# A second feed-forward stage whose token loads, weight loads and one subtraction are issued elsewhere

## The chip, the cores and the metric

The kernel runs on one core of one Trainium2 chip. The metric is the device time of one execution in microseconds (us). Three executions of the kernel before took 1824.18, 1825.57 and 1827.65 us; the median is 1825.57 us.

## The reference

Three stages follow each other. Attention over 8 x 8 heads with keys and values averaged in groups of 8 gives 4608 token vectors of 512 numbers. A first feed-forward network (512 to 2048 to 512) follows. The second one, around which the change lies, is:

```python
rms = np.sqrt(np.mean(x * x, axis=-1, keepdims=True) + 1e-06)
xn = x / rms * rms_g
g = xn @ w_gate
silu = g * (1.0 / (1.0 + np.exp(-g)))
val = xn @ w_val
return (silu * val @ w_out).astype(np.float32)
```

Here x is 4608 x 512, w_gate and w_val are 512 x 1536 and w_out is 1536 x 512, all in float32.

## The kernel before

Every float32 operand of a matmul is split into a high and a low part (helper `split`, L88 to L95: the high part is a copy on ScalarE, the low part a subtraction on an engine that the caller names), and a product is three matmuls.

The second network starts some 980 us into the span and treats the tokens in five pairs of two token blocks: pairs 0, 2 and 4 with 512 tokens in a block, pairs 1 and 3 with 384. For a pair, the products with w_gate ("g") and w_val ("v") are done by twelve **quads** (class `Quad`): six pairs of column blocks p, each first for g and then for v. A quad multiplies 2 x 2 blocks with seven block products (Strassen's scheme) in the steps p1, p6, p5, p2, p7, p4, p3; each step is six matmuls. p1 of the next quad is put ahead of p4 and p3. A quad uses three banks of PSUM: x (p1, p2), y (p6, p7, p4) and w (p5, p3). Results leave the banks through VectorE and ScalarE; in a g quad ScalarE applies Silu, in a v quad VectorE and GpSimd multiply and split.

The product with w_out (`out_part`, L1089) is cut in **pieces**, two for each of its twelve row blocks f and each token block z. Those of z = 0 are put between the quads' steps by `piece()`, one behind p7 and one behind p3; those of z = 1 follow the last quad, and the last four of them go into the first two quads of the next pair. Four banks take the sums; the copies out (`oe`) must leave a bank before z = 1 writes it.

Weights come from device memory, all issued by the SyncE queue (SP), in order: an instruction whose buffer is not yet left holds up all that is behind it. A quad needs four tiles `a` (`load_a`, L956) out of ten slots: tile 0 is read by p1 and p2, tile 1 by p6 and p5, tile 2 by p7 and p3, tile 3 by p4. So in quad i the load of a tile ten further on takes the slot of a tile of quad i. w_out comes as tiles `wo` (`load_o`, L966) in four slots, issued by a piece three blocks ahead of its use.

While a pair is being multiplied, the next pair's tokens are loaded and normalised in small steps (`norm_steps`), one behind each of p6, p5, p2 and p7 (`between`). For each of its two blocks z: `load` (tile `xst`, L832), four `square` (ScalarE, sums on GpSimd into `acc`, L844 to L848), `mean` (`acc` split into the tile `ahl`), empty steps, `root` (two matmuls `ms` with a matrix of ones, L857, then Sqrt on ScalarE, L860, which changes ScalarE's function table and back), `inverse` (VectorE, L864) and `scaled` (VectorE, L868). For the first pair the same steps run in the last tile of the first network, four at a time.

Within the second network every engine executes in the order in which the code issues (a chain of dependencies, L1220 on, sees to it); in the first network a scheduler may reorder.

Of the kernel before, what the change touches and what calls it, by code (L numbers as in the profile page):

```python
# [16 lines left out]
HI, LO = 0, 1  # L17
# [5 lines left out]
def pooled_attention_then_two_ffns(  # L23
# [13 lines left out]
    nc = tc.nc  # L37
# [6 lines left out]
    KC = DM // P  # L44
# [24 lines left out]
    def bank(tag, bufs, name):  # L69
        return ps.tile([P, 512], F32, tag=tag, bufs=bufs, name=name)  # L70
# [18 lines left out]
    def split(hi_eng, hi, lo_eng, lo, src):  # L89

        if hi_eng is nc.scalar:
            nc.scalar.activation(out=hi, in_=src, func=AF.Copy)  # L92
        else:
            hi_eng.tensor_copy(out=hi, in_=src)
        lo_eng.tensor_tensor(out=lo, in0=src, in1=hi.bitcast(F32), op=ALU.subtract)  # L95
# [11 lines left out]
    class Weights:  # L107
# [51 lines left out]
        def step(self):  # L159
            if self.begun:  # L160
                self.end()
            while self.todo and len(self.loaded) < self.ahead(self.todo[0]):
                self.load()
            if self.loaded:
                self.begin()
# [640 lines left out]
    def slot(kind, i, name):  # L806

        base, n = {
            "t": (0, T_SLOTS), "a": (T_SLOTS, A_SLOTS), "o": (T_SLOTS + A_SLOTS, O_SLOTS),
            "u": (T_SLOTS + A_SLOTS + O_SLOTS, F2),  # L810
        }[kind]
        return weight_slot(free2[base + i % n], name)

    def norm_steps(q):

        t0, n = pairs[q]
        xs = []
        steps = []

        def wait():  # L820
            pass

        for z in range(2):
            ta = t0 + z * n

            def load(z=z, ta=ta):
                x = p2.tile([P, KC, N], F32, tag="xst", bufs=2, name=f"xst{q}_{z}")[:, :, :n]
                xs.append(x)
                at_ = ta
                while at_ < ta + n:  # L830
                    end = min(ta + n, (at_ // N + 1) * N)
                    nc.sync.dma_start(  # L832
                        out=x[:, :, at_ - ta:end - ta],
                        in_=y_dram[at_ // N][:, :, at_ % N:at_ % N + end - at_],
                    )
                    at_ = end

            held = {}

            def square(c, z=z, held=held):  # L840
                x = xs[z]
                if c == 0:
                    held["acc"] = p2.tile([P, N], F32, tag="acc", bufs=1, name=f"acc{q}_{z}")[:, :n]
                    nc.scalar.activation(out=held["acc"], in_=x[:, c, :], func=AF.Square)  # L844
                else:
                    s = per.tile([P, N], F32, tag="tg", bufs=3, name=f"sq{q}_{z}_{c}")[:, :n]
                    nc.scalar.activation(out=s, in_=x[:, c, :], func=AF.Square)
                    nc.gpsimd.tensor_tensor(out=held["acc"], in0=held["acc"], in1=s, op=ALU.add)  # L848

            def mean(z=z, held=held):  # L850
                held["a"] = p2.tile([P, 2, N], F32R, tag="ahl", bufs=1, name=f"ahl{q}_{z}")[:, :, :n]
                split(nc.scalar, held["a"][:, HI, :], nc.gpsimd, held["a"][:, LO, :], held["acc"])

            def root(z=z, held=held):
                pt = bank("h", 2, f"ms{q}_{z}")[:, :n]
                for i in range(2):
                    nc.tensor.matmul(pt, ones, held["a"][:, i, :], start=i == 0, stop=i == 1)  # L857
                r = p2.tile([P, N], F32, tag="rms", bufs=1, name=f"rms{q}_{z}")[:, :n]
                held["r"] = r
                nc.scalar.activation(out=r, in_=pt, func=AF.Sqrt, bias=eps)  # L860

            def inverse(c, held=held):
                r = held["r"]
                nc.vector.reciprocal(out=r[:, c:c + P], in_=r[:, c:c + P])  # L864

            def scaled(c, z=z, held=held):
                x = xs[z]
                nc.vector.scalar_tensor_tensor(  # L868
                    out=x[:, c, :], in0=x[:, c, :], scalar=gain[:, c:c + 1], in1=held["r"],
                    op0=ALU.mult, op1=ALU.mult,  # L870
                )

            steps.insert(z, load)

            steps += [wait] + [lambda c=c, f=square: f(c) for c in range(KC)] + [mean, wait, wait, root, wait]
            steps += [lambda c=c, f=inverse: f(c) for c in range(0, n, P)]
            steps += [lambda c=c, f=scaled: f(c) for c in range(KC)]
        return xs, steps
# [67 lines left out]
    def load_a():  # L946
        if a_count[0] < len(a_todo):
            i = a_count[0]
            a_count[0] += 1
            if len(a_todo[i]) == 3:  # L950
                load_o_into(a_todo[i], "a", i)
                return
            q, p, m, s = a_todo[i]
            t = slot("a", i, f"a{m}{q}_{p}_{s}")
            k = 2 if s < 3 else 1
            nc.sync.dma_start(  # L956
                out=t.rearrange("p h n -> p (h n)")[:, :k * 512].bitcast(F32),
                in_=op_dram[m, p][:, s, 0:k].rearrange("p a c n -> p (a c n)"),
            )
            a_tiles[q, p, m, s] = t.rearrange("p h n -> p (h n)").rearrange(  # L960
                "p (a c h n) -> p a c h n", a=2, c=2, h=2
            )

    def load_o_into(key, kind, i):
        t = slot(kind, i, f"wo{key[0]}_{key[1]}_{key[2]}")
        nc.sync.dma_start(out=t.bitcast(F32), in_=wo_dram[key[2]])  # L966
        o_tiles[key] = t
# [6 lines left out]
    def first_pair():  # L974

        xs, norm = norm_steps(0)
        early, late = token_steps(0, xs)
        when = {}
        for i, x in enumerate(norm):
            when.setdefault(i // 4, []).append(x)  # L980
        first = (len(norm) - 1) // 4 + 1
        for i, x in enumerate(early):
            when.setdefault(first + i, []).append(x)
        for i in range(A_SLOTS):
            when.setdefault(10 + i // 2, []).append(load_a)
        for i in range(3):
            when.setdefault(13 + i // 2, []).append(load_o)
        return when, late
# [173 lines left out]
    def piece():  # L1162
        if pieces:
            pieces.pop(0)()

    def queue_out(q, z, f):
        for ms in ((0, 1), tuple(range(2, pairs[q][1] // P))):
            def one(ms=ms):
                if ms[0] == 0:
                    load_o()  # L1170
                    if (q, z) == (last_q, 1):
                        load_a()
                out_part(q, z, f, ms)
            pieces.append(one)

    begun = len(nc.cur_bb.bb.instructions)
    for q, (_, n) in enumerate(pairs):
        quads = [Quad(q, p, m) for p in range(NPAIR) for m in "gv"]
        more = q + 1 < len(pairs)
        xs, norm = norm_steps(q + 1) if more else (None, [])  # L1180

        def between():
            load_a()
            if norm and i >= 2:
                norm.pop(0)()

        for i, a in enumerate(quads):
            if i == 0:
                a.p1()
            for step in (a.p6, a.p5, a.p2, a.p7):  # L1190
                step()
                between()
            piece()
            if i + 1 < len(quads):
                quads[i + 1].p1()
            a.p4()
            a.p3()

            if i + 1 < (len(quads) if more else len(quads) - 2):
                piece()  # L1200
            if a.m == "v":
                for f in (2 * a.p, 2 * a.p + 1):
                    queue_out(q, 0, f)
        assert not norm
        while pieces:
            piece()
        for f in range(F2):
            queue_out(q, 1, f)
        early, late = token_steps(q + 1, xs) if more else ([], [])

        for i in range(len(pieces) - (4 if more else 0)):
            if i % 3 == 0 and early + late:
                (early or late).pop(0)()
            piece()
        assert not early + late
# [40 lines left out]
```

## Time and profile before

| | |
|---|---|
| median of three runs | 1825.57 us |
| the profiled execution | 1826.16 us |
| its span, first to last instruction | 1824.4 us |
| TensorE matmul busy (PE) | 1764.8 us, 97% |
| VectorE (DVE) / ScalarE (ACT) / GpSimd (POOL) busy | 881.1 / 669.4 / 557.0 us |
| DMA moved | 330.81 MB, mean 181 GB/s |
| mean granted TensorE clock | 0.992 |

The first three rows say that a term read in the trace can be taken off the profiled execution's own time, 1.8 us above its span and 0.6 us above the median. PE is busy nearly always; the busy time of a matmul runs into that of the next, so a wait shows best in the distance between the starts of two steps. The second network takes the last 843 us of the span.

### The profile page before, as it was taken

How to read it: one execution, taken by the hardware profiler on the slowest of the kernel's cores; microseconds unless marked ns; L12 is line 12 of the kernel's file. 1: busy time of each engine (PE TensorE's matmuls, PEld its weight loads, DVE VectorE, ACT ScalarE, POOL GpSimd, SP SyncE). 2: the span in 40 equal slices, each digit the busy share in tenths (PEclk: the TensorE clock that was granted, in tenths of full speed). 3: DMA queues.
4: the chain of work that ended last, by engine and by line, in shares of the span. 5: the costliest groups of instructions: out<-in, count | busy, mean ns of one | idle time of the engine just before them, and what ended most of it. 6: DMA issues, size and time to landing. Idle time of an engine off the chain costs nothing.

```text
span 1824.4 us, 23632 instructions
## 1 busy us (share of the span) xinstructions
PE 1764.8 (97%) x8596; PEld 1504.5 (82%) x8596; DVE 881.1 (48%) x1593; ACT 669.4 (37%) x1424; POOL 557.0 (31%) x691
## 2 busy tenths in 40 slices
PE   4899999999999999999999999999999999999999
PEld 3789887888888887888888878989787888988887
DVE  8974445463356555554244336344534533463331
ACT  5754334343343444343433332233232223322220
POOL 2653204243124252111211442244144114513330
PEclk9999999999999999999999999999999999999999
DMA  8832105446365445445442657687676567776562
GB/s 266 292 118 85 47 21 159 151 150 222 104 192 161 157 147 161 144 143 165 159 150 82 230 175 247 188 294 245 237 248 207 187 221 281 247 264 201 197 208 104
DMA packets 175556, 330.81 MB, mean 181 GB/s; under 512 B 54352, under 2 KB 90192, under 8 KB 174928
## 3 DMA queue, kind: packets, MB, share of 16 engines
q1 hardware_dynamic: 175440, 329.31, 54.9%
q8 instruction: 68, 1.11, 0.3%
q14 instruction: 48, 0.39, 0.1%
HBM read 277.87 MB, written 51.38 MB: 180 GB/s over the span
## 4 chain that ended last, share of the span: by engine, by line
PE 87%; DVE 4%; DMA 4%; POOL 2%; issue 1%; ACT 1%; SPq 1%; ACTq 0%; DVEq 0%; POOLq 0%
PE h L592 20%; PE y L628 20%; PE o L1089 14%; PE yv L1014 6%; PE yg L1014 6%; PE xv L1014 4%; PE wv L1014 4%; PE wg L1014 4%; PE xg L1014 4%; PE sc L325 2%; DMA wo<-wo 1%; PE av L395 1%; DMA xst<-y 1%; PE xt L369 1%; PE qt L303 1%
## 5 line engine op out<-in xcount | busy, mean ns | idle before, releaser
L592 PE MATMUL h<-xhl,w_i 128*128 128x512 f32 (+1 forms) x1824 | 438.6, 386 | 3.0 <-ACT xhl L92 1.5
L592 PEld LDWEIGHTS h<-xhl,w_i 128*128 128x128 f32 x1824 | 330.3, 191 | 67.7 <-DVE xhl L95 3.2
L1089 PE MATMUL o<-wo,u 128*128 128x512 f32 x1296 | 315.7, 391 | 5.1 <-DMA wo<-wo 5.1
L1089 PEld LDWEIGHTS o<-wo,u 128*128 128x128 f32 x1296 | 243.0, 188 | 54.1 <-issue 4.3
L628 PE MATMUL y<-ghl,w_o 128*128 128x512 f32 (+1 forms) x1296 | 285.1, 365 | 1.4 <-DVE ghl L605 1.4
L628 PEld LDWEIGHTS y<-ghl,w_o 128*128 128x128 f32 x1296 | 219.0, 191 | 35.1 <-DVE ghl L605 1.8
L605 DVE TENSOR_TENSOR ghl<-g,ghl 128x512 fp32r<-128x512 f32 (+1 forms) x152 | 114.5, 754 | 245.1 <-ACT g L98 241.9
L98 ACT ACTIVATE ghl<-h 128x512 fp32r<-128x512 f32 (+1 forms) x152 | 86.9, 572 | 227.6 <-PE h L592 227.1
L628 PE MATMUL y<-ghl,wr 128*128 128x512 f32 x624 | 158.6, 395 | 0.0
L628 PEld LDWEIGHTS y<-ghl,wr 128*128 128x128 f32 x624 | 115.1, 188 | 22.4
L95 POOL TENSOR_TENSOR u<-e2g,u 128x512 fp32r<-128x512 f32 (+1 forms) x25 | 29.6, 1182 | 287.1 <-ACT u L92 277.7
L229 POOL TENSOR_TENSOR v<-v 128x256 f32<-128x256 f32 (+2 forms) x84 | 61.3, 733 | 111.1 <-DMA v<-in_v_dram 108.5
L1014 PE MATMUL xv<-xa,av 128*128 128x512 f32 (+1 forms) x360 | 85.8, 374 | 6.1 <-ACT e1v L1042 6.1
L98 ACT ACTIVATE g<-h 128x512 f32<-128x512 f32 (+1 forms) x152 | 86.7, 571 | 0.0
L1014 PE MATMUL yv<-T,av 128*128 128x512 f32 (+1 forms) x360 | 85.3, 373 | 0.0
L1014 PE MATMUL yg<-T,ag 128*128 128x512 f32 (+1 forms) x360 | 83.9, 368 | 0.0
L1014 PE MATMUL xg<-xa,ag 128*128 128x512 f32 (+1 forms) x360 | 83.8, 368 | 0.0
L1014 PEld LDWEIGHTS xv<-xa,av 128*128 128x128 f32 x360 | 67.5, 192 | 16.2 <-ACT e1v L1042 6.7
L1014 PEld LDWEIGHTS yv<-T,av 128*128 128x128 f32 x360 | 67.8, 192 | 9.5
L1014 PEld LDWEIGHTS xg<-xa,ag 128*128 128x128 f32 x360 | 66.2, 188 | 9.5
L1014 PEld LDWEIGHTS yg<-T,ag 128*128 128x128 f32 x360 | 66.2, 188 | 9.4
L735 POOL TENSOR_TENSOR parts_g<-raw_g,parts_g 128x256 fp32r<-128x256 f32 (+1 forms) x48 | 33.6, 723 | 100.1 <-ACT parts_g L731 100.1
(166 smaller groups left out, 2594.8 us busy)
## 6 DMA issues: line engine op xcount, KB each, us to landing
wo<-wo SPq DMA_DIRECT2D x120, 512.0 KB
av<-op_v SPq DMA_DIRECT2D x90, 512.0 KB
ag<-op_g SPq DMA_DIRECT2D x90, 512.0 KB
wr<-wo SPq DMA_DIRECT2D x52, 512.0 KB
y<-ye SPq DMA_DIRECT2D x36, 256.0 KB
op_g<-parts_g SPq DMA_DIRECT2D x36, 256.0 KB
op_v<-parts_v SPq DMA_DIRECT2D x36, 256.0 KB
out_dram<-oe SPq DMA_DIRECT2D x36, 256.0 KB
```

The source lines that it names most:

```text
L95: lo_eng.tensor_tensor(out=lo, in0=src, in1=hi.bitcast(F32), op=ALU.subtract)
L98: return nc.scalar.activation(out=out, in_=in_, func=AF.Prelu, scale=scale, alpha=alpha)
L229: nc.gpsimd.tensor_tensor(out=x[:, :n], in0=x[:, :n], in1=x[:, n:2 * n], op=ALU.add)
L303: nc.tensor.transpose(pt[:, c * P:(c + 1) * P], x[:, c * P:(c + 1) * P], ident)
L325: nc.tensor.matmul(pt[:, i * n:(i + 1) * n], y[:, p, :], kblk[b % 2][:, p * n:(p + 1) * n], start=True, stop=True,)
L369: nc.tensor.transpose(pt[:, c * P:(c + 1) * P], e[:, c, 0:P], ident)
L592: nc.tensor.matmul(pt, w[:, sp, c * P:(c + 1) * P], x[:, mp, c, :], start=c == 0 and i == 0, stop=c == n_k - 1 and i == 2,)
L605: nc.vector.tensor_tensor(out=t[:, LO, :], in0=g, in1=t[:, HI, :].bitcast(F32), op=ALU.subtract)
L628: nc.tensor.matmul(pt, w[:, sp, m * P:(m + 1) * P], g[:, mp, a - c0:a - c0 + n], start=ydone[j, a] == 1 and i == 0 and m % per_bank == 0, ...
L735: own(nc.gpsimd.tensor_tensor(out=d[:, :, LO, :], in0=x, in1=d[:, :, HI, :].bitcast(F32), op=ALU.subtract))
L1014: nc.tensor.matmul(pt, wt[:, a, c, sp, :], xt[:, mp, :], start=start and c == 0 and i == 0, stop=c == 1 and i == 2, skip_group_check=not s ...
L1089: nc.tensor.matmul(pt, u[:, sp, m * P:(m + 1) * P], w[:, mp, :], start=f == 0 and i == 0, stop=f == F2 - 1 and i == 2,)
```

## The change

Four edits. `mean` names VectorE instead of GpSimd for the low part of `ahl`. In `norm_steps` the empty step moves from ahead of the squares to behind them. `between` no longer issues weight loads, and hands out the two `load` steps behind p6 and p5 of quad 1 (before: quad 2); the other steps start with quad 2. Two `load_a` stand behind p2 and two behind p3 (before: one behind each of p6, p5, p2 and p7).

```diff
--- before.py
+++ after.py
@@ -849,7 +849,7 @@
 
             def mean(z=z, held=held):
                 held["a"] = p2.tile([P, 2, N], F32R, tag="ahl", bufs=1, name=f"ahl{q}_{z}")[:, :, :n]
-                split(nc.scalar, held["a"][:, HI, :], nc.gpsimd, held["a"][:, LO, :], held["acc"])
+                split(nc.scalar, held["a"][:, HI, :], nc.vector, held["a"][:, LO, :], held["acc"])
 
             def root(z=z, held=held):
                 pt = bank("h", 2, f"ms{q}_{z}")[:, :n]
@@ -872,7 +872,7 @@
 
             steps.insert(z, load)
 
-            steps += [wait] + [lambda c=c, f=square: f(c) for c in range(KC)] + [mean, wait, wait, root, wait]
+            steps += [lambda c=c, f=square: f(c) for c in range(KC)] + [wait, mean, wait, wait, root, wait]
             steps += [lambda c=c, f=inverse: f(c) for c in range(0, n, P)]
             steps += [lambda c=c, f=scaled: f(c) for c in range(KC)]
         return xs, steps
@@ -1178,23 +1178,29 @@
         quads = [Quad(q, p, m) for p in range(NPAIR) for m in "gv"]
         more = q + 1 < len(pairs)
         xs, norm = norm_steps(q + 1) if more else (None, [])
+        n_norm = len(norm)
 
         def between():
-            load_a()
-            if norm and i >= 2:
+            if norm and (i >= 2 or i == 1 and len(norm) > n_norm - 2):
                 norm.pop(0)()
 
         for i, a in enumerate(quads):
             if i == 0:
                 a.p1()
+
             for step in (a.p6, a.p5, a.p2, a.p7):
                 step()
                 between()
+                if step == a.p2:
+                    load_a()
+                    load_a()
             piece()
             if i + 1 < len(quads):
                 quads[i + 1].p1()
             a.p4()
             a.p3()
+            load_a()
+            load_a()
 
             if i + 1 < (len(quads) if more else len(quads) - 2):
                 piece()
```

SP's queue in pair 1, quads 1 and 2, before. `ag_2_0` is tile 0 of the g quad of p = 2, `av` the same for v, `wo_0_2` the tile of z = 0, f = 2, `oe` a result going out, `xst_0` and `xst_1` the tokens of pair 2 (the pair's number is left out of these names):

```order
L956 DMA ag_2_0_10697<-op_g_344 128x1024
L956 DMA ag_2_1_10712<-op_g_344 128x1024
L966 DMA wo_0_2_10714<-wo_356 128x1024
L1100 DMA out_dram<-oe_1_0_10719 128x512
L1100 DMA out_dram<-oe_1_1_10725 128x512
L1100 DMA out_dram<-oe_1_2_10762 128x512
L1100 DMA out_dram<-oe_1_3_10768 128x512
L956 DMA ag_2_2_10780<-op_g_344 128x1024
L832 DMA xst_0_10782<-y_93 128x4x256
L832 DMA xst_0_10782<-y_94 128x4x256
L956 DMA ag_2_3_10792<-op_g_344 128x512
L832 DMA xst_1_10794<-y_94 128x4x256
```

The same queue with the change, from the end of quad 0:

```order
L956 DMA av_1_0_10657<-op_v_349 128x1024
L956 DMA av_1_1_10659<-op_v_349 128x1024
L832 DMA xst_0_10676<-y_93 128x4x256
L832 DMA xst_0_10676<-y_94 128x4x256
L832 DMA xst_1_10686<-y_94 128x4x256
L832 DMA xst_1_10686<-y_95 128x4x256
L956 DMA av_1_2_10699<-op_v_349 128x1024
L956 DMA av_1_3_10701<-op_v_349 128x512
L966 DMA wo_0_2_10716<-wo_356 128x1024
L1100 DMA out_dram<-oe_1_0_10721 128x512
L1100 DMA out_dram<-oe_1_1_10727 128x512
```

The token loads stand a quad earlier, behind two weight tiles whose slots quad 0 has left, and no longer behind `ag_2_2`, whose slot quad 2's own p2 has to leave.

SP in the last quad of pair 1, before:

```order
L956 DMA av_0_2_11587<-op_v_348 128x1024
L956 DMA av_0_3_11597<-op_v_348 128x512
L956 DMA ag_1_0_11610<-op_g_343 128x1024
L956 DMA ag_1_1_11625<-op_g_343 128x1024
L966 DMA wo_1_0_11627<-wo_354 128x1024
L966 DMA wo_1_1_11660<-wo_355 128x1024
```

With the change:

```order
L956 DMA av_0_2_11606<-op_v_348 128x1024
L956 DMA av_0_3_11608<-op_v_348 128x512
L966 DMA wo_1_0_11623<-wo_354 128x1024
L956 DMA ag_1_0_11653<-op_g_343 128x1024
L956 DMA ag_1_1_11655<-op_g_343 128x1024
L966 DMA wo_1_1_11660<-wo_355 128x1024
```

`wo_1_0`, the first tile that z = 1 needs, has moved ahead of `ag_1_0` and `ag_1_1`, whose slots are left by p3 and p4 of this last quad.

GpSimd in pair 0, quad 7 (a v quad, p = 3), before; `acc` is the sum of squares of block z = 1, `u` are the split products:

```order
L848 TENSOR_TENSOR acc_1_9901<-acc_1_9901,sq_1_1_9912 128x384
L95 TENSOR_TENSOR u_1_6_9922<-e2g_3_9834,u_1_6_9922 128x512
L848 TENSOR_TENSOR acc_1_9901<-acc_1_9901,sq_1_2_9927 128x384
L1030 TENSOR_TENSOR e7g_3_9845<-e7v_3_9936,e7g_3_9845 128x512
L95 TENSOR_TENSOR u_2_7_9940<-e7g_3_9845,u_2_7_9940 128x512
L848 TENSOR_TENSOR acc_1_9901<-acc_1_9901,sq_1_3_9945 128x384
L1030 TENSOR_TENSOR e1g_3_9776<-e1v_3_9866,e1g_3_9776 128x512
L95 TENSOR_TENSOR u_1_7_9973<-e1g_3_9776,u_1_7_9973 128x512
L1030 TENSOR_TENSOR e6g_3_9813<-e6v_3_9897,e6g_3_9813 128x512
L95 TENSOR_TENSOR u_2_6_9984<-e6g_3_9813,u_2_6_9984 128x512
L95 TENSOR_TENSOR ahl_1_10004<-acc_1_9901,ahl_1_10004 128x384
```

GpSimd with the change, from the same quad's start:

```order
L848 TENSOR_TENSOR acc_1_9825<-acc_1_9825,sq_1_1_9835 128x384
L848 TENSOR_TENSOR acc_1_9825<-acc_1_9825,sq_1_2_9852 128x384
L848 TENSOR_TENSOR acc_1_9825<-acc_1_9825,sq_1_3_9907 128x384
L95 TENSOR_TENSOR u_1_6_9924<-e2g_3_9833,u_1_6_9924 128x512
L1030 TENSOR_TENSOR e7g_3_9848<-e7v_3_9940,e7g_3_9848 128x512
L95 TENSOR_TENSOR u_2_7_9944<-e7g_3_9848,u_2_7_9944 128x512
```

VectorE with the change, same quad:

```order
L991 TENSOR_TENSOR e6v_3_9905<-yv_3_9898,e1v_3_9870 128x512
L1030 TENSOR_TENSOR e2g_3_9833<-xv_3_9863,e2g_3_9833 128x512
L95 TENSOR_TENSOR ahl_1_9927<-acc_1_9825,ahl_1_9927 128x384
L991 TENSOR_TENSOR e7v_3_9940<-yv_3_9898,e1v_3_9870 128x512
L991 TENSOR_TENSOR e7v_3_9940<-wv_3_9910,e7v_3_9940 128x512
L991 TENSOR_TENSOR e1v_3_9870<-yv_3_9898,e1v_3_9870 128x512
L991 TENSOR_TENSOR e6v_3_9905<-wv_3_9910,e6v_3_9905 128x512
```

The sums now stand ahead of the quad's products, and the low part of `ahl` has gone from the end of GpSimd's list to VectorE, between the multiplication behind p2 (L1030) and the additions behind p7 (`e7v`). The `root` of this block has moved from behind p7 to behind p5 of quad 8; in pairs 1 and 3 from behind p6 of quad 9 to behind p2 of quad 8.

## Rows read from the trace of the kernel before

**Rows 1.** Waits of TensorE: who for whom, us in total, times, longest.
```profile
PE xv L1014 <- ACT e1v L1042: 6.1, 2, 3.5
PE o L1089 <- DMA wo<-wo: 5.1, 4, 2.6
PE ms L857 <- POOL ahl L95: 2.9, 2, 1.5
```

**Rows 2.** Windows: stretch; us; busy PE, PEld, DVE, ACT, POOL; PE clock; DMA share, GB/s.
```profile
1520.00:1530.00 10.00, 7.43 (x25) 6.63 (x24) 2.23 (x4) 3.91 (x8) 4.68 (x4) 0.66 1.00 408
```

**Rows 3.** Timeline of PE, pair 1: start, length, what, [idle before, releaser].
```profile
1171.55 1.20 PE L1014 MATMUL wv<-T,av 128*128 128x384 f32 x6
...
1176.06 1.21 PE L1014 MATMUL xg<-xa,ag 128*128 128x384 f32 x6
...
1191.01 1.20 PE L1014 MATMUL wv<-T,av 128*128 128x384 f32 x6
...
1195.71 2.29 PE L1014 MATMUL xv<-xa,av 128*128 128x384 f32 x6 [3.49 <-ACT e1v L1042]
...
1200.78 1.23 PE L1014 MATMUL xg<-xa,ag 128*128 128x384 f32 x6
```

**Rows 4.** Timeline of PE, pair 3, the same two steps.
```profile
1520.09 1.20 PE L1014 MATMUL wv<-T,av 128*128 128x384 f32 x6
...
1530.27 1.23 PE L1014 MATMUL xg<-xa,ag 128*128 128x384 f32 x6
```

**Rows 5.** Timeline of SP and ACT, pair 1, quads 0 to 2.
```profile
1169.31 0.79 SPq L956 DMA_DIRECT2D av<-op_v  x2
...
1184.83 1.82 SPq L832 DMA_DIRECT2D xst<-y  x2
...
1194.66 0.63 ACT L844 ACTIVATE acc<-xst 128x512 f32<-128x512 f32 x1 [7.94 <-DMA xst<-y]
```

**Rows 6.** Chain that ended last: start, us, link.
```profile
1185.63 8.95 DMA xst<-y
...
1280.15 5.82 DMA wo<-wo
```

**Rows 7.** Timeline, all engines, pair 0, quad 8, steps p2 and p7.
```profile
1078.54 1.52 PE L1014 MATMUL xg<-xa,ag 128*128 128x512 f32 x6
...
1079.89 1.52 PE L1014 MATMUL yg<-T,ag 128*128 128x512 f32 x6
...
1080.89 0.51 ACT L92 ACTIVATE ahl<-acc 128x384 fp32r<-128x384 f32 x1
...
1082.25 0.69 DVE L991 TENSOR_TENSOR e7g<-wg,e7g 128x512 f32<-128x512 f32 x1
...
1082.29 1.00 POOL L95 TENSOR_TENSOR ahl<-acc,ahl 128x384 fp32r<-128x384 f32 x1
...
1083.35 0.44 PE L857 MATMUL ms<-ahl,ones 128*128 128x384 f32 x1 [1.45 <-POOL ahl L95]
...
1083.62 1.28 ACT L860 ACT_TABLE_LOAD   x1
1083.62 1.55 PE L1089 MATMUL o<-wo,u 128*128 128x512 f32 x6
```

**Rows 8.** Timeline, SP, DVE and PE, end of pair 1's quads.
```profile
1279.12 4.96 PE L1089 MATMUL o<-wo,u 128*128 128x512 f32 x21
...
1279.31 0.79 SPq L956 DMA_DIRECT2D ag<-op_g  x2
...
1280.15 2.24 SPq L966 DMA_DIRECT2D wo<-wo  x3
...
1283.59 1.28 DVE L1098 COPY oe<-o 128x512 f32<-128x512 f32 x2
...
1286.11 14.11 PE L1089 MATMUL o<-wo,u 128*128 128x512 f32 x61 [2.03 <-DMA wo<-wo]
```

**Rows 9.** Instructions on tile xst: VectorE's low part, ns min/median/max.
```profile
L95 DVE TENSOR_TENSOR xa<-xst,xa x15: 551/681/1775, 919.2 to 1620.1; 128x512 fp32r<-128x512 f32 x9, 128x384 fp32r<-128x384 f32 x6
```

## The prediction

> **What bounds the kernel now.** The first page shows PE busy nearly all the time, so I went from it to the waits of TensorE. In the second network only three of them are worth a sum [rows 1]: steps of x in v quads wait twice for a ScalarE copy (6.1 us), the product with w_out waits four times for a transfer (5.1 us), and the mean's matmul waits twice for GpSimd (2.9 us). These are idle times alone; what each really costs I read from the distance between the starts of the same two steps with and without the wait.
>
> First wait, pairs 1 and 3. From the start of wv (p5) to the start of the next quad's xg lie 4.51 us in an undisturbed quad (1171.55 to 1176.06), but 9.77 us at 1191.01 [rows 3]: 5.26 us lost. In pair 3 it is 10.18 us [rows 4]: 5.67 us lost. Both are more than the idle time because the granted clock falls behind the wait: 0.66 of full in the stretch from 1520 to 1530, between the levels 2.4 and 1.2 GHz [rows 2]. The cause stands on the other queues [rows 5]. ScalarE has been idle for 7.94 us when, at 1194.66, the first square can read xst; the copy e1v, for which PE waits, is queued behind it. The load had been issued only at 1184.83, and the chain of waits has it at 8.95 us [rows 6].
>
> Second wait, pairs 0 and 2, quad 8. A step of six takes 1.35 us (1078.54 to 1079.89), the two matmuls of 384 columns would take 2/6 x 384/512 of that, 0.34. So the next product was due at 1081.58; it started at 1083.62: 2.04 us lost [rows 7]. GpSimd's subtraction at 1082.29 ends last, although ScalarE's high part was there from 1080.89 on: GpSimd is still at the quad's splits.
>
> Third wait, the turn from z = 0 to z = 1. In pair 1 PE has 21 matmuls left at 1279.12, 4.73 us of work, and goes on at 1286.11 instead of 1283.85: 2.26 us lost. SP issued the two ag tiles at 1279.31, when their slots came free, and only then wo_1_0, at 1280.15 [rows 8]; it needed 5.82 us [rows 6]. The longest wait of this kind is 2.6 us, in pair 3; with the same 0.23 beside the idle time that is 2.83 us. The other two are what is left of 5.1: 0.5 us together [rows 1].
>
> **The change part by part.** *Token loads a quad sooner.* They now follow quad 0's last weight pair, in pair 1 issued at 1169.31 and for 0.79 us: so xst_0 at about 1170.1. With the old time from issue to use, 1184.83 to 1194.66, 9.83 us [rows 5], it is there at 1179.9. The squares are asked for three steps earlier; ScalarE came to them at 1186.72 (1194.66 less 7.94), so now at about 1183.5, three steps of 1.05 before (4.51 less a piece of 1.36, by three). 3.6 us to spare, and PE needs nothing from ScalarE's queue until the xv step due at about 1192. Both stalls go: 5.26 + 5.67 = 10.93 us. What is late next there: nothing that I can find. The weight tiles queued behind xst are used two quads later, about 20 us. Cost 0; as a bound, half of the 10.93 comes back if the landing takes more than twice as long, since weights and results now travel beside it.
>
> *Mean's low part on VectorE, squares two or three steps sooner.* In quad 7 the three sums now stand ahead of GpSimd's products, so ahl is complete most of a quad before its matmul: 2 x 2.04 = 4.08 us go. The price is a place in VectorE's queue, in front of the additions that free bank y for p4. In pairs 0 and 2 VectorE's part behind p2 is: multiplication 0.69, ScalarE's split 0.63 (as its copy of that size [rows 5]) and ahl copy 0.51, the low part at most 0.69 (median 0.681 [rows 9]), then the addition 0.69 [rows 7]: 3.2 us, some 3.4 with the hand-overs, against three steps (p7, a piece, p1), 4.05 us. In pairs 1 and 3 the mean stands behind p7, in front of p4's addition, and by the same rows about half a microsecond remains. So 0; from below not under 0, since these additions wait for PE anyway; from above 0.5 for each of the four tight places, 2 us.
>
> *Weights where their slots are left.* A weight tile is issued at the same moment as before, because the slot decided then too. What gains is all that stood behind a waiting tile: wo_1_0 goes out behind p2 of the last quad, three steps and a piece earlier, and lands before 1283.85. Late next is the bank: VectorE's two copies at 1283.59 take 0.64 each, so the first bank of z = 1 is free at 1284.23, with the hand-over 1284.3: 0.45 us of each stall stays. wo_1_1 takes the old place of wo_1_0, issued at 1280.15 and there by 1285.97 [rows 6, 8], and is needed nine matmuls after 1284.3, at 1286.3. So 2.26 - 0.45 + 2.83 - 0.45 + 0.5 = 4.7 us go. Bounds: 3 us if wo_1_1 is a microsecond late in both pairs, 5.6 if no bank waits.
>
> *Roots moved.* In pairs 0 and 2 the root of z = 1 now precedes Silu of p2, so two table loads of 1.28 us [rows 7] lie in front of the copy that frees bank x. Counted from GpSimd's last split of quad 7, bank x is free about when the next p1 wants it. I take 0.2 us each, 0.4; bounds 0 and 1.3 (one load) each.
>
> *First network's last tile.* The same steps run there, with a few places exchanged; PE does not wait there for them, and ahl's low part finds VectorE idle. 0.
>
> Sum: 10.93 + 4.08 + 4.7 - 0.4 = 19.3 us. The profiled execution took 1826.16 us, so 1806.9; as it lies 0.6 us above the median, I say 1806.8.
>
> **A rule that speaks against it.** The low part on VectorE reads two tiles. Such instructions took 0.551 to 1.775 us here, with a median of 0.681 [rows 9]. So one can be held up by 1.09 us, and more GpSimd work lies beside VectorE in a v quad than anywhere else.
> The Trainium skill, "SBUF - State Buffer", section "Who interferes with whom", says why: a VectorE instruction with two SBUF inputs and a GpSimd one that reads SBUF exclude each other, and the second waits for the first to finish. The spread in the row agrees; it does not name the GpSimd instruction.
>
> **The rivals.**
> *The hold-up is the rule, not the exception.* Each of the four tight low parts (z = 1 of pairs 0 to 3) takes 1.775. The margin of 0.6 us in pairs 0 and 2 leaves 0.5 of stall, that of 0.5 in pairs 1 and 3 leaves 0.6: 2.2 us, 1809. For it the maximum of the row; against it the median.
> *The tokens come late again.* The same 16 DMA engines are full where the old load ran (share 1.00 in [rows 2]). If xst needs twice its 9.83 us from 1170.1, it is there at 1189.8, still before 1192; it must need over 22 us to give back half: 1812. Against it: the load now lies in a stretch in which less is asked for.
> *Slower: VectorE held by the mean.* Eight low parts stand in front of additions that PE needs. If ahl's copy came as late against its new place as it now comes against the root (1080.89, 0.7 us before the matmul was due [rows 7], three to four steps behind the mean's place), VectorE would stand some 5 us each time; less the margin of 0.6, 8 x 4.4 = 35 us, and the sum becomes 1842. It decides at 19.3/8 = 2.4 us of stall each. Against it: the sums' last addition now starts two steps before the mean, and takes 1.0 us, as GpSimd's low part of the same size.
> *It does not do what it says.* SP still finds the tokens' buffers taken, or another wait takes each place: 1824. Against it: the buffers of xst are read for the last time before quad 0.
>
> **How the numbers follow.** Forecast 0.71, hold-up 0.12, late tokens 0.08, no effect 0.04, slower 0.05. A measurement of this kernel tells 0.2% (3.7 us) from no change: faster by more 0.91, within 0.04, slower by more 0.05. The range goes down to 1804, for banks and tables that cost nothing (1.3 us) and small waits that I did not price, and up to 1813, which takes in the first two rivals; 0.1 is left out.
>
> **What will show it.** Right: no wait of xv for e1v, clock 1.00 in all windows of the second network, ms without a wait, xst issued at about 1170 and there by 1180, wo_1_0 issued ahead of the two ag tiles and a rest of about 0.5 us at the turn to z = 1. Wrong: PE steps p4 or p6 that wait for VectorE's additions behind an ahl subtraction; p1 of quad 9 that waits for Silu; weights that come late behind xst.

## The result, and the profile after

The changed kernel takes 1809.57 us (median of six executions, 1804.95 to 1812.26), the kernel before in the same session 1825.37 us (six, 1822.30 to 1831.46). The ratio is 0.9907, 95% interval 0.9890 to 0.9924: faster by 15.8 us. Forecast were 1806.8 us, that is 19.3 us less.

A time alone does not tell which terms hold, so I cut the second network of both traces at the first xg of each pair (us):

| pair | before | after | gained | forecast |
|---|---|---|---|---|
| 0 | 177.77 | 175.26 | 2.51 | 2.04 + 0.25 - 0.2 = 2.1 |
| 1 | 147.25 | 142.07 | 5.18 | 5.26 + 1.81 = 7.1 |
| 2 | 181.82 | 179.32 | 2.50 | 2.04 + 0.25 - 0.2 = 2.1 |
| 3 | 148.23 | 142.60 | 5.63 | 5.67 + 2.38 = 8.0 |
| 4 | 184.12 | 184.15 | 0.0 | 0 |
| sum | 839.19 | 823.40 | 15.8 | 19.3 |

Pair 4 ends with the last matmul. The gain of 15.8 us in the second network is as large as that of the medians. The two profiled executions differ by less, 1826.16 and 1812.26, mostly because the second network began at 981.61 in the one and at 983.16 in the other. The sums of the last two columns are worked from unrounded terms. All that is missing, and a little more, is missing in pairs 1 and 3. One trace is one execution: in a second trace of the same kernel (the control below) pairs 0, 2 and 4 come out the same within 0.02 us, but pairs 1 and 3 take 141.70 and 142.00, so that its sum is 822.41. Differences of 1 us between single traces therefore prove little.

The waits of TensorE in the trace after; columns: who waited for whom, us in total, times, longest. Of the three waits of [rows 1] one is left, and of it two occurrences instead of four:

```profile
PE o L1089 <- DMA wo<-wo: 3.4, 2, 2.0
```

**The tokens.** The timeline of SP, ScalarE and PE after, pair 1, quads 0 to 2 (start, us, what), against [rows 3, 5]:

```profile
1169.25 2.71 SPq L832 DMA_DIRECT2D xst<-y  x4
...
1182.61 0.63 ACT L844 ACTIVATE acc<-xst 128x512 f32<-128x512 f32 x1
...
1186.41 0.48 ACT L1042 COPY e1v<-xv 128x384 f32<-128x384 f32 x1
...
1190.06 1.20 PE L1014 MATMUL wv<-T,av 128*128 128x384 f32 x6
...
1194.57 1.21 PE L1014 MATMUL xg<-xa,ag 128*128 128x384 f32 x6
```

The loads go out at 1169.25 and not at 1184.83. The first square, 13.4 us later, has no wait in brackets, where 7.94 us stood. The copy e1v follows it at 1186.41, and from wv to xg it is 4.51 us, the distance of an undisturbed quad, where 9.77 stood. In pair 3 it is 4.51 as well, and the fallen clock of [rows 2] is gone: it is 1.00 in all of the second network from 980 to 1800. The window of that place (busy us of PE, PEld, DVE, ACT, POOL, then granted clock, DMA share and GB/s) reads:

```profile
1510.00:1520.00 10.00, 10.00 (x56) 9.51 (x55) 4.38 (x8) 2.54 (x6) 4.07 (x4) 1.00 0.90 306
```

**The mean.** Pair 0, all engines, quad 7 and quad 8 after, against [rows 7]:

```profile
1070.84 1.30 POOL L95 TENSOR_TENSOR u<-e2g,u 128x512 fp32r<-128x512 f32 x1 [3.95 <-ACT u L92]
1071.21 1.34 DVE L95 TENSOR_TENSOR ahl<-acc,ahl 128x384 fp32r<-128x384 f32 x1 [1.11 <-ACT ahl L92]
1071.92 1.52 PE L1014 MATMUL xg<-xa,ag 128*128 128x512 f32 x6
1072.47 0.68 DVE L991 TENSOR_TENSOR e7v<-yv,e1v 128x512 f32<-128x512 f32 x1
...
1073.29 1.58 PE L1014 MATMUL yv<-xb,av 128*128 128x512 f32 x6
...
1080.16 0.51 PE L857 MATMUL ms<-ahl,ones 128*128 128x384 f32 x2
...
1082.49 1.28 ACT L860 ACT_TABLE_LOAD   x1
...
1083.79 0.58 ACT L860 ACTIVATE rms<-ms,eps 128x384 f32<-128x384 f32 x1
...
1084.39 1.28 ACT L1023 ACT_TABLE_LOAD   x1
1084.60 1.54 PE L1014 MATMUL xv<-xa,av 128*128 128x512 f32 x6
1085.68 0.60 ACT L1023 ACTIVATE e2g<-xg 128x512 f32<-128x512 f32 x1
```

ahl is whole at 1072.55, 7.6 us ahead of its matmuls, which start without a wait. Two of my worries stand here to be seen. VectorE's subtraction took 1.34 us; the quickest of these took 0.548 in the same trace. It began while GpSimd's at 1070.84 was still running, and the next addition, e7v, started on its heels; yet p4 (yv) came at 1073.29, one step of 1.36 behind xg, because e7v had read its bank by 1073.15. And the two table loads do hold Silu of p2 (e2g) back to 1085.68, but p1 of the next quad (xv, 1084.60) did not wait for it. In the kernel's code x and ms share two banks (`bank("h", 2, ...)`): xv starts before Silu has read xg, so it has taken the other bank, which Sqrt (1083.79, 0.58 us) had just left.

**The turn from z = 0 to z = 1.** Pair 1, SP, DVE, PE and its weight loads (PEld) after, against [rows 8], and the last row from the chain that ended last (start, us, link), against [rows 6]:

```profile
1269.40 0.43 SPq L966 DMA_DIRECT2D wo<-wo  x1
1273.01 11.66 PE L1089 MATMUL o<-wo,u 128*128 128x512 f32 x48
1273.20 0.79 SPq L956 DMA_DIRECT2D ag<-op_g  x2
...
1274.09 2.19 SPq L966 DMA_DIRECT2D wo<-wo  x2
...
1277.48 1.28 DVE L1098 COPY oe<-o 128x512 f32<-128x512 f32 x2
...
1278.02 1.91 PEld L1089 LDWEIGHTS o<-wo,u 128*128 128x128 f32 x9 [0.47 <-ACT oe L1096]
...
1278.19 1.35 SPq L1100 DMA_DIRECT2D out_dram<-oe  x3
...
1279.63 19.33 SPq L966 DMA_DIRECT2D wo<-wo  x10
...
1280.30 3.95 PEld L1089 LDWEIGHTS o<-wo,u 128*128 128x128 f32 x18 [0.36 <-DMA wo<-wo]
...
1286.08 14.12 PE L1089 MATMUL o<-wo,u 128*128 128x512 f32 x61 [1.41 <-DMA wo<-wo]
```

```profile
1279.63 6.40 DMA wo<-wo
```

wo_1_0 is issued ahead of the two ag tiles, as forecast, and PE runs on through the first 48 matmuls: the 21 that were left of z = 0, and 27 of z = 1, three tiles of nine. Then it waits for the fourth, wo_1_3. At 0.2267 us each (a sixth of a step of 1.36 us) the 48 end at 1283.89, so 2.19 us are lost; by the same 0.2267 the kernel before lost 2.23. 1.41 of the 2.19 are this wait, and some 0.2 are the difference between loss and idle time that stood beside the wait before too. The rest lies among the 48: 0.3 at 1278.0, where z = 1 waits for a bank that a copy of z = 0 leaves, and 0.2 at 1280.3, where wo_1_1 is a little late. The slot of wo_1_3 was that of the last wo tile of z = 0, left some 21 matmuls after 1273.01, at 1277.8. But on SP three results stand ahead of the load, and they wait for VectorE's copies at 1277.48: the load goes out at 1279.63, 1.8 us late, and takes 6.40 us. In pair 3 it is the same: the wait is 1.95 us, the loss 2.74 us where 2.79 were.

### The profile page after: what moved, and what is told of

Read it like the earlier page. It is cut to its first block, busy times and chain, and to the rows that moved or that the text cites. A ratio compares the mean times of both kernels' runs of the same rounds, so it can differ in the third digit from the quotient of the medians.

```text
span 1810.5 us, 23634 instructions
## 1 busy us (share of the span) xinstructions
PE 1758.0 (97%) x8596; PEld 1498.0 (83%) x8596; DVE 891.1 (49%) x1603; ACT 670.4 (37%) x1424; POOL 551.2 (30%) x681
## 3 DMA queue, kind: packets, MB, share of 16 engines
q8 instruction: 68, 1.11, 0.3%
## 4 chain that ended last, share of the span: by engine, by line
PE 89%; DVE 5%; DMA 3%; issue 1%; ACT 1%; SPq 1%; POOL 1%; ACTq 0%; DVEq 0%; POOLq 0%
PE y L628 20%; PE h L592 20%; PE o L1089 16%; PE yg L1014 6%; PE yv L1014 6%; PE xv L1014 4%; PE xg L1014 4%; PE wg L1014 4%; PE wv L1014 4%; PE sc L325 2%; PE av L395 1%; PE xt L369 1%; DMA wo<-wo 1%; PE qt L303 1%; DMA y<-ye 1%
```

## The experiments

The kernels below ran in three groups, each on one chip beside the kernel before, whose median was 1824.36 us for the first four kernels, 1825.09 for the next three and 1824.3 for the last three. "Network" is the sum of the table above for the one trace that was kept of each kernel (before 839.19, after 823.40).

**Each edit by itself.** Theory: three separate stalls, so three separate gains. Rival: one edit pays and the others ride on it.

Weights alone:

```diff
         def between():
-            load_a()
             if norm and i >= 2:
...
                 step()
                 between()
+                if step == a.p2:
+                    load_a()
+                    load_a()
...
             a.p3()
+            load_a()
+            load_a()
```

> The kernel before with the weight loads alone moved (two behind p2, two behind p3). Theory: a quad sooner is what removed the token stalls, so here they stay in part. xst_0 of pair 1 is no longer behind ag_2_2, but still behind the results of quad 1, which SP stored until 1183.1 with the whole change: issued at about 1183.2 instead of 1184.83, 1.6 us sooner, so the wait of xv for e1v falls from 3.5 to about 2 us in pair 1 and from 2.6 to about 1 in pair 3. The ms wait (2 x 1.45) stays; the turn to z = 1 keeps its loss in pairs 1 and 3, now in front of wo_1_3 instead of wo_1_0. About 1820 us. Rival: the freed queue alone carries it; xv waits no more, about 1813.

Measured 1818.94 us, ratio 0.9968 (0.9956 to 0.9980); network 831.34, 7.9 less than before. The waits of PE:

```profile
PE o L1089 <- DMA wo<-wo: 4.3, 3, 2.3
PE ms L857 <- POOL ahl L95: 2.9, 2, 1.5
PE xv L1014 <- ACT e2g L1023: 2.1, 2, 1.1
PE xv L1014 <- ACT e1v L1042: 0.5, 1, 0.5
```

The time came out as expected, by another way: moving only the weights already lets the tokens out at 1180.58 instead of 1184.83, because they no longer stand behind a tile whose slot is not left, and the wait for e1v falls from 6.1 to 0.5 us, where I had expected about 3 to stay. But p1 of a later quad then waits for Silu of p2 (e2g): 2.1 us of a wait that neither the kernel before nor the one after has. ScalarE and PE in pair 1 (start, us, what):

```profile
1203.04 0.52 ACT L92 ACTIVATE u<-e6g 128x384 fp32r<-128x384 f32 x1 [2.10 <-POOL e6g L1030]
1203.47 0.47 ACT L1023 ACTIVATE e2g<-xg 128x384 f32<-128x384 f32 x1
...
1203.96 1.28 ACT L860 ACT_TABLE_LOAD   x1
...
1204.00 1.31 PE L1014 MATMUL xv<-xa,av 128*128 128x384 f32 x6 [1.10 <-ACT e2g L1023]
```

The root's table load is not the cause, it comes behind Silu. Silu is late because ScalarE first waits 2.10 us for GpSimd's product e6g, and in GpSimd's queue the low part of ahl (1.29 us at 1198.12) lies ahead of that product; no run here takes it out with the rest unchanged. This part of the change is worth more for the tokens than for the turn.

Tokens alone:

```diff
+        norm[2:2] = [lambda: None] * 2 if more else []
+        n_norm = len(norm)
...
-            if norm and i >= 2:
+            if norm and (i >= 2 or i == 1 and len(norm) > n_norm - 2):
```

> The kernel before with the token loads alone moved to quad 1 (two empty steps keep all other steps where they were). xst_0 of pair 1 stands behind av_1_2, which waits for quad 1's p2, so it is issued at about 1173.7 and lands some 9.8 us later, about 1183.5, before ScalarE comes to the squares at 1186.7. Theory: no wait of xv for e1v, 10.9 us gained, 1814.5 us; ms wait 2.9 us and the turn's waits of about 5 us stay. Rival, the DMA engines are as full there: it lands after 1192 and about half of the stall stays, 1820 us.

Measured 1815.71 us, ratio 0.9956 (0.9941 to 0.9971); network 830.23, 9.0 less. No wait for e1v is left: the term of 10.93 us holds, since pair 3 gains 5.85 (0.13 of it is a shorter wait at the turn, 2.46 for 2.59). Pair 1 gains only 3.44, and the reason stands at the turn, where the clock falls behind a wait of 2.30 us (PE's timeline, then windows with the granted clock):

```profile
1283.44 22.27 PE L1089 MATMUL o<-wo,u 128*128 128x512 f32 x90 [2.30 <-DMA wo<-wo]
```

```profile
1284.20:1286.00 1.80, 1.80 (x6) 1.41 (x5) 0.96 (x2) 0.77 (x2) 0.06 (x1) 0.50 1.01 391
1286.00:1287.60 1.60, 1.60 (x5) 1.23 (x4) 1.19 (x1) 1.43 (x3) 1.33 (x2) 0.50 1.07 425
```

The same 90 matmuls took 20.69 us in the trace of before at full clock. So the wait cost 1.6 us more than its length. This is one execution, 4.2 us above the median of its kernel.

Mean alone:

```diff
-                split(nc.scalar, held["a"][:, HI, :], nc.gpsimd, held["a"][:, LO, :], held["acc"])
+                split(nc.scalar, held["a"][:, HI, :], nc.vector, held["a"][:, LO, :], held["acc"])
-            steps += [wait] + [lambda c=c, f=square: f(c) for c in range(KC)] + [mean, wait, wait, root, wait]
+            steps += [lambda c=c, f=square: f(c) for c in range(KC)] + [wait, mean, wait, wait, root, wait]
```

> The kernel before with the low part of ahl on VectorE and the empty step behind the squares, nothing else. The mean stays behind p6 of quad 8 in pairs 0 and 2, so ScalarE's copy comes as late as before (1080.9) but VectorE subtracts at once instead of GpSimd behind its splits: the loss at ms falls from 2.04 to about 0.6 us in each of the two pairs. Theory: 3 us gained, about 1822.5 us, token stalls and turn unchanged. Rival, VectorE is held by the mean: a new wait of PE for VectorE, not faster than 1825.4 us.

Measured 1827.78 us, ratio 1.0019 (1.0006 to 1.0033): slower. Its waits, and ScalarE and PE in pair 1 when the late tokens come:

```profile
PE xv L1014 <- ACT e1v L1042: 7.5, 2, 4.0
PE yg L1014 <- DVE e7g L991: 1.7, 2, 0.8
PE ms L857 <- DVE ahl L95: 0.6, 2, 0.3
```

```profile
1191.41 0.63 ACT L844 ACTIVATE acc<-xst 128x512 f32<-128x512 f32 x1 [9.78 <-DMA xst<-y]
1191.94 0.51 ACT L1023 ACTIVATE e7g<-e7g 128x384 f32<-128x384 f32 x1
...
1192.87 0.46 ACT L1042 COPY e1v<-xv 128x384 f32<-128x384 f32 x1
...
1193.38 2.29 PE L1014 MATMUL xv<-xa,av 128*128 128x384 f32 x6 [3.99 <-ACT e1v L1042]
```

The wait for the mean falls from 2.9 to 0.6, as expected; but a square that is asked for a step earlier, while its tokens are as late as ever, holds ScalarE for 9.78 us and has a Silu more behind it. The wait for e1v grows from 6.1 to 7.5 us, and in pairs 1 and 3 VectorE's low part delays the additions (1.7 us), which is the rival of the expectation. Pairs 0 and 2 do gain, 1.40 and 1.62 us. In the trace the clock also falls behind the turn's wait of 2.25 us in pair 3: its 90 matmuls take 22.27 us for 20.68 before, so 1.6 us of what this trace lost are the clock's. My expectation took the term of 4.08 as independent of the loads, and missed. The medians change by -5.42, -8.65 and +3.42 us, together -10.65, against -15.8 for the whole change; the network times of single traces, -7.9, -9.0 and +2.1, make -14.7. The sums differ too much to size what the edits owe to each other. But an edit that alone is slower, and with the two others takes away 2 x 1.96 us, pays only once the tokens are early.

**The engine of the low part.** Is it VectorE that takes the mean's wait away, or the squares that come sooner?

```diff
-                split(nc.scalar, held["a"][:, HI, :], nc.vector, held["a"][:, LO, :], held["acc"])
+                split(nc.scalar, held["a"][:, HI, :], nc.gpsimd, held["a"][:, LO, :], held["acc"])
```

> The whole change, with the low part of ahl back on GpSimd. Theory: the earlier place of sums and mean removed the ms wait, not the engine; GpSimd subtracts in quad 7 behind one split, a quad before ms wants it. ms does not wait, same time as the whole change, about 1809.6 us. Rival: the engine mattered; ms waits about 1.45 us again in pairs 0 and 2, 4 us slower, about 1813.6 us.

Measured 1808.79 us, ratio 0.9916 (0.9901 to 0.9932); network 821.99. No wait for the mean, and the interval overlaps that of the whole change (0.9890 to 0.9924): the engine is worth nothing that can be measured here, the order of the steps is what counts. At the turn this trace waits 1.53 us in pair 1, in front of wo_1_1, and 0.52 in pair 3, in front of wo_1_3.

**The wait at the turn.** Theory from the trace after: wo_1_3 is late because three results stand ahead of it. Rival: it is late because its transfer is slow, whenever it is issued. The control is the changed kernel once more:

> The whole change once more, as the measure for the two that follow on the same chip: 1809.6 us, turn to z = 1 in pairs 1 and 3 with a wait of 1.4 and 2.0 us in front of wo_1_3.

Measured 1808.17 us (1807.12 to 1809.93), ratio 0.9903 (0.9887 to 0.9919); network 822.41. It waits 1.26 and 1.02 us in front of wo_1_3, and 0.22 in front of wo_1_1 in pair 3: 2.5 us, less than the 3.4 of the first trace.

Results of z = 0 kept back until the next load of wo is issued (`store()` issues what was kept):

```diff
-                nc.sync.dma_start(out=out[r:r + P, :], in_=t)
+                stores.append(lambda r=r, t=t: nc.sync.dma_start(out=out[r:r + P, :], in_=t))
+                if z:
+                    store()
...
                     load_o()
+                    if z:
+                        store()
```

> The whole change, and the results of z = 0 are stored behind the next wo load instead of ahead of it. Theory: the wait at the turn is SP's order: wo_1_3 stood behind three stores that wait for the copies out of the banks, issued at 1279.63 although its slot was left at about 1277.7; now issued at 1277.8, 1.8 us sooner. PE's wait for wo falls from 1.4 and 2.0 us to under 0.4 in pairs 1 and 3; what is left is the bank, 0.6 each. 3.4 us faster than the whole change, about 1806.2 us. Rival, the 16 DMA engines are full there and it lands when the bytes ahead of it are through: unchanged, 1809.6 us.

Measured 1806.14 us (1804.13 to 1808.32), ratio 0.9894 (0.9880 to 0.9909); network 820.96. The waits of PE (the first row), SP and PE in pair 1:

```profile
PE o L1089 <- DMA wo<-wo: 1.2, 2, 0.8
```

```profile
1271.43 7.38 PE L1089 MATMUL o<-wo,u 128*128 128x512 f32 x30
1272.52 4.23 SPq L966 DMA_DIRECT2D wo<-wo  x3
1276.84 1.40 SPq L1100 DMA_DIRECT2D out_dram<-oe  x3
...
1279.20 18.69 PE L1089 MATMUL o<-wo,u 128*128 128x512 f32 x81 [0.38 <-DMA wo<-wo]
```

Three wo tiles, not two, now stand ahead of the results, and the waits fall from 2.5 us in the control to 1.2. I had expected less than 0.4 in each pair; pair 1 kept 0.38 and pair 3 kept 0.84. Neither is a wait for wo_1_3: 30 matmuls end with wo_1_0, so pair 1 waits for wo_1_1, and pair 3 waits behind 57, for wo_1_4. The first matmul of wo_1_3 comes late by 0.2 to 2.5 us in all eight turns of the four traces that have the changed order of weights and the results ahead of the load (the weights alone, the kernel after, the control and the low part on GpSimd), and in none of the ten turns of the five traces in which the load stands ahead of the results (this kernel, its repetition and the three built on it, all below). So the order on SP is shown as the cause of that wait, and not as the only thing that makes a wo tile late. The device times of control and edit overlap; the network is 1.45 us shorter. The 1806.2 us of the expectation were met by luck: the step was to be 3.4 us, and it is 2.0 from a control that was itself quicker than expected.

Is the rest the two ag tiles, whose transfers run beside those of wo? Issued behind piece 9 of z = 1, on top of the edit above:

```diff
-            load_a()
-            load_a()
+            if i + 1 < len(quads) or not more:
+                load_a()
+                load_a()
...
             piece()
+            if more and i == 9:
+                load_a()
+                load_a()
```

> As the kernel with the later stores, and the two weight tiles behind p3 of a pair's last quad (1 MB, needed two quads into the next pair) are issued after ten pieces of z = 1 instead. If transfers share the engines, wo_1_1 to wo_1_3 land sooner and no wait for wo is left: about 1805.4 us. If the time from issue to landing does not depend on the load beside it: as the kernel with the later stores, 1806.2 us. If the ag tiles then come late in the next pair: a new wait of xg or yg for them.

Measured 1808.9 us (1807.51 to 1811.43), ratio 0.9910 (0.9896 to 0.9924); network 823.23: a miss. The tiles only push the next wo tiles back (SP and PE, pair 1):

```profile
1284.30 0.90 SPq L956 DMA_DIRECT2D ag<-op_g  x2
1284.39 8.45 PE L1089 MATMUL o<-wo,u 128*128 128x512 f32 x36 [0.49 <-DMA wo<-wo]
1294.17 4.42 PE L1089 MATMUL o<-wo,u 128*128 128x512 f32 x18 [1.33 <-DMA wo<-wo]
```

Behind piece 17 no wo tile of z = 1 is left to push (the same edit with 17 in place of 9):

> The stores of z = 0 go out late as in the kernel with the later stores, and the two tiles of ag that the last quad issues at the turn of a pair are issued only behind piece 17 of z = 1, when every wo piece of z = 1 has been issued. Theory (what is left of the wait for wo at the turn is the transfers of wo sharing the DMA engines with ag): the waits for wo at the turns of pairs 1 and 3 fall from 1.2 us in all to below 0.4, nothing takes their place, pairs 1 and 3 shorten by about 0.5 us each, and the time is 1805.0 us. Rival (the transfers of wo are late by themselves, one piece after another, whatever else is in flight): the waits stay at about 1.2 us and the time at 1806.1. Second rival (the two ag tiles now come late, as they did behind piece 9): a wait for ag or wo of 0.5 to 1.5 us appears at the first quad of the next pair, and the time is 1807 to 1809.

Measured 1805.48 us (1802.04 to 1808.07), ratio 0.9892 (0.9872 to 0.9911); network 820.29. The waits for wo are 0.7 us in all (0.31 and 0.38, both in front of wo_1_4), between the theory's 0.4 and the rival's 1.2.

And the bank copies, with the engines of z = 0 exchanged on top of it:

```diff
-                if m % 2:
+                if (m + 1 - z) % 2:
                     nc.scalar.copy(out=t, in_=pt)
```

> As the kernel with the last weights behind piece 17, and the copies of the z = 0 banks change engines (the first and third on ScalarE, the second on VectorE, so that the first bank doesn't wait behind VectorE's split of the last gate). Theory (some 0.5 us at each of the turns of pairs 1 and 3, 0.3 at those of pairs 0 and 2, are the bank copies): 0.3 to 0.5 us less in each of pairs 1 and 3, time about 0.6 to 1 us below the run with the copies as they were. Rival (the banks are waited for because the last product has only just ended, whichever engine copies): the same time within 0.3 us.

Measured 1805.44 us (1802.20 to 1807.16), ratio 0.9895 (0.9878 to 0.9913); network 819.96. In pair 1 the 57 matmuls up to the wait take 13.14 us where they took 13.47 in the kernel before it, and the wait is longer, 0.76 for 0.31:

```profile
1269.60 13.14 PE L1089 MATMUL o<-wo,u 128*128 128x512 f32 x57
1283.50 12.56 PE L1089 MATMUL o<-wo,u 128*128 128x512 f32 x54 [0.76 <-DMA wo<-wo]
```

The wait for the bank, 0.3 us, is gone in both pairs, so the copies are its cause. What it gives back the transfer takes in pair 1: that is 140.86 us long, 140.80 without this edit. Pair 3 did gain 0.47, so over both the theory's size is not reached and the rival's nought not shown. The waits for wo are 1.0 us in all.

The base for these two, the kernel with the later results again on the same chip:

> The kernel with the later stores once more, unchanged, as the base for the two others on the same chip: 1806.1 us, waits for wo 1.2 us in all.

Measured 1804.74 us (1802.75 to 1806.75), ratio 0.9891 (0.9874 to 0.9908); waits for wo 1.1 us. The three can't be told apart. The kernel with the later results has the lower median than the control, 1806.14 against 1808.17, and beats the kernel before by about 19 us; the two further edits add nothing that the time shows.

## Why the prediction was right, and where not

*Tokens: right in mechanism and size.* 10.93 us forecast; the wait for e1v is gone, the distance is 4.51 us again, and pair 3 of the kernel with the tokens alone gained 5.85 us against 5.67. That xst would be there by 1180 no row shows, only that it was there by 1182.61. Transfers beside the weights did not make them late: from issue to first use it is 13.4 us, and the use had no wait.

*Mean: right.* 2 x 2.04 us; pairs 0 and 2 gained 2.5 each. Of that their turns make 0.55, by the kernel with the weights alone (177.22 and 181.28 us), which leaves 1.96 for the mean. That VectorE does it made no difference (1808.79 and 1808.17 us with GpSimd and with VectorE).

*VectorE held up: the mechanism is there, the price is not.* I gave 0.12 to a low part of 1.775 us; it took 1.34. The margin of 0.6 us that I worked out covered it, with 0.14 us to spare (1073.15 to 1073.29). The Trainium skill, "SBUF — State Buffer", section "Who interferes with whom", has a VectorE instruction with two SBUF inputs and a GpSimd one that reads SBUF exclude each other. The rows agree: the subtraction that began inside GpSimd's took 1.34 us for the 0.548 of the quickest.

*Roots: 0.4 forecast, 0 measured, by a wrong reading.* I took it that the table loads "lie in front of the copy that frees bank x". The Silu that they hold back is late, but the next p1 takes the other bank, the one that Sqrt leaves 0.23 us before (1084.37 to 1084.60). The wait for Silu in the kernel with the weights alone is not of this kind, since Silu stands ahead of the table loads there.

*The turn: the step that failed.* "So 2.26 - 0.45 + 2.83 - 0.45 + 0.5 = 4.7 us go." That wo_1_0 comes in time was right. But for the loads I priced wo_1_0 and wo_1_1 and stopped. The fourth tile, wo_1_3, stands on SP behind three results that wait for the bank copies; with the first wait gone PE came to it before its data, and lost 2.19 and 2.74 us where it had lost 2.23 and 2.79. In pairs 1 and 3 the term brought 0.1 us of 4.2; the two other turns brought 1.1 for the 0.5 forecast: some 1.2 of 4.7. The runs show the place: with the results behind the load the waits fall from 2.5 us to 1.2, and none of them is for wo_1_3 any more. With the ag tiles out of the way as well they are 0.7 and 1.0, which the time does not show. The bank that I left at 0.45 us cost 0.3. My lower bound of 3 us thought of one tile a microsecond late, which did happen to wo_1_1 in two other traces (1.53 us with the low part on GpSimd, 1.11 with the weights alone), and not of a queue in which a result may stand ahead of a load.

Of 19.3 us forecast 3.5 are missing at the turns and the roots' 0.4 come back: 16.2, for 15.8 measured. The rest, some 0.1 us in each of the first four pairs, I did not trace.

## What to carry to other kernels

When a load is brought forward on a queue that issues in order, follow the queue to the next instruction that waits for something else, and price the loads behind it too: the wait does not vanish, it moves to them. Edits that each take away a stall are not additive if one only brings a step earlier whose input another one must bring: ask of every moved instruction what stands behind it on its engine while it waits. And a gain of 2 us in a kernel whose second network began between 976.22 and 983.16 us in traces of kernels that are alike up to there is read from the stretch of the trace that it touches, not from one time.

## What the hardware did that I had not expected

A stall's length alone does not say whether the clock falls behind it. The turns of pairs 1 and 3 hold seven waits of more than 2 us of the product with w_out, in the traces of the kernel before and of the three with one edit each. Behind two of them, 2.30 us (tokens alone, pair 1) and 2.25 us (mean alone, pair 3), the granted clock fell to 0.50, the lower of the two levels of 1.2 and 2.4 GHz; with the tokens alone it stood there from about 1284.2 to 1287.6. The 90 matmuls took 22.27 us both times. Behind 2.03, 2.27, 2.32, 2.46 and 2.59 us the matmuls kept their full pace. The longest, 2.59 us, is that of the kernel before in pair 3, which ran on at full clock (PE's timeline, and the window behind it):

```profile
1616.16 20.68 PE L1089 MATMUL o<-wo,u 128*128 128x512 f32 x90 [2.59 <-DMA wo<-wo]
```

```profile
1616.00:1618.00 2.00, 1.84 (x8) 1.56 (x9) 1.54 (x3) 0.36 (x1) 0.00 (x0) 1.00 0.99 389
```

So I would now price a stall of this size with a range: its length, and up to 1.6 us on top. What decides between the two no run here was made to show.
